# A windowed-attention kernel with two feed-forward layers: the softmax's sum, constant, reciprocal and division of a strip ordered ahead of the next strip's maximum and GpSimd pass in iterations -1 to 9

## The chip, the core and the metric

One core of a Trainium2 chip. The core has five engines with queues of their own, each run in order: TensorE (matrix products, PE in the profile; PEld are its weight loads), VectorE (DVE), ScalarE (ACT), GpSimd (POOL) and SyncE (SP), which here issues all the DMAs. The metric is the time of one execution on the device in microseconds.

## What is computed

Attention over 2 batches, 8 heads, 768 positions with head size 64, then two feed-forward layers over the 1536 resulting rows of 512 with 2048 hidden units. Cut to what matters:

```
k_sum, v_sum = max and mean of k and v over blocks of 32 positions
local  = q k^T / 8 where |i - j| < 16, else -1e9
blocks = q k_sum^T / 8 + log(32)
a = exp([local, blocks] - max);  a = a / (sum(a) + 1e-9)
x = a [v, v_sum]
h = x w_in1;  g = max(h, 0) + alpha * min(h, 0);  x = g w_out1
h = x w_in2;  g = P(h) / (Q(h) + 1e-6);           out = g w_out2
```

## The kernel before, in words

The 2 x 768 queries are cut into 24 strips of 64. A strip's scores, for four pairs of heads at once, are a tile of 128 x 480: 96 local keys and 24 block keys per pair. One iteration of the loop over t (-1 to 27) issues for several strips the steps that a pipeline has them at. The dictionary `attn` gives each step's offset: `qk`, `mask` (scores into SBUF, L402), `max` (L410) and `sub` (subtraction of the maximum, L415, only for strips marked "s" in `SOFTMAX`) work on strip t; `exp` (L420 or L424), `sum` (L429, where ScalarE has not summed already), `guard` (the constant 1e-9, L434 or L436), `inv` (reciprocal, L440) and `norm` (the division as a product, L444) on strip t-1; `turn` (transposes on TensorE, L450) and `turned` (their copy to SBUF, `pT`) on strip t-2 and `vm`, `pv` (product with v, L464), `out` and `outl` (x as a high part `xh` and a rest `xl`, L478) on strip t-3 (from strip 8 on, one iteration later in each). `k` copies the keys of strip t+1 into `kc`.

Between these stand the steps of the first feed-forward layer: `H` (products `h`, L195) from iteration 6 on, `act` (its activation in three pieces, on ScalarE and VectorE: relu L204, factor L137, L208), `gh` and `gl` (a high part and a rest of its result), and `Y` (L258). Weights come as 64-bit words by DMA into `raw` and are split on the way: `new` (`top` on ScalarE, L161), `low` (`cv` on VectorE, L163, after which the next piece's DMA is issued), `hi` (copy on ScalarE), `mid` and `end` (the two halves of the rest `wil` or `wol`, on GpSimd, L173). `top` is one buffer, so the next `top` waits for the `cv` that reads it. The buffers in PSUM of the scores, the transposes and the product with v are single.

The order inside an iteration is written out by hand: `ORDERS` has one list of steps for each stage, and `PHASES` (3, 5, 7, 10, 14) says at which iteration the next list begins. `ENG` has one letter per stage and step for the engine: v VectorE, a ScalarE, p GpSimd. A step's instructions go to the end of their engine's queue; what they wait for is added by the framework from the tiles that they read and write. Behind the loop, from about 145 us on, a second loop runs the rest of both layers.

```python
            for step in ORDERS[sum(t >= at for at in PHASES)].split():
                if step in attn:
                    f, o = attn[step]
                    for n in {t + o, t + o - (o < -1)}:
```

Of the kernel before, what the change touches and what calls it, by code (L numbers as in the profile page):

```python
# [39 lines left out]

PHASES = (3, 5, 7, 10, 14)
ORDERS = (
    ("qk mask k act mid exp max turn gl vmean sum kmax vm end ks out hi low pv inv sub outl Y norm guard turned "
     "v act in act H gh new"),
    ("act qk sum hi mid turn act vm act mask in exp vmean gh gl max pv ks v guard out inv sub low turned k end Y "
     "outl kmax H new norm"),
    ("qk vm exp hi act mask pv mid sum max out Y turn sub inv gl guard in low outl act v vmean k act norm H "
     "turned new ks end kmax gh"),
    ("gh qk act pv ks act act exp out end mask hi k sum gl max vmean outl low kmax turn guard mid Y v vm in sub "
     "inv new turned H norm"),  # L50
    ("ks act end act gh exp qk pv hi out mid v act mask k sum gl max outl sub turn vmean Y kmax low H turned in "
     "new inv vm guard norm"),
    ("vm act act gh act qk exp mask hi sum max pv gl inv sub out k mid v outl in turn turned vmean kmax new low "
# [4 lines left out]

SOFTMAX = 'aaaassasaasssabssssssass'

ENG = {"guard": "vapppv", "k": "vaaaaa", "turned": "aaaaaa", "vm": "aaapaa", "ks": "ppppav", "norm": "vppppp", "sub": "pppppp",
       "gl": "vvvppp", "gh": "vapaaa", "hi": "vaaaaa", "mid": "pvpppp", "end": "pppppp", "out": "aaaaaa", "al": "vavaaa"}

LEAD = (4, 6, 4, 4, 9, 13, 5, 10)
# [6 lines left out]
def kernel(  # L71
# [59 lines left out]
    def eng(step):  # L131
        return {"a": nc.scalar, "v": nc.vector, "p": nc.gpsimd}[ENG[step][sum(now[0] >= t for t in PHASES)]]

# [588 lines left out]
```

## Time and profile before

| | us |
|---|---|
| median of 3 runs | 621.86 (621.47 to 623.15) |
| profiled execution | 620.94 |
| its span, first to last instruction | 618.8 |
| TensorE busy | 594.4 (96%) |
| ScalarE busy | 383.7 (62%) |
| GpSimd busy | 354.8 (57%) |
| VectorE busy | 338.9 (55%) |

Times in the trace count from the start of the span. Busy TensorE is not TensorE at its peak, since its products are pipelined. A row of the timeline gives the start, the duration, the engine, the line, the operation, the tile written and those read, and in square brackets the engine's idle time just before, with what ended it.

### The profile page before, as it was taken

Reading aid. Unit: us, or ns where it says so; the run is one execution under the profiler, and the core shown is the slowest. Engines: PE = TensorE matmul, PEld = TensorE weight load, DVE = VectorE, ACT = ScalarE, POOL = GpSimd, SP = SyncE. Lnnn points to the kernel's source line nnn. Section 1 sums busy time; section 2 is a strip of 40 time slices with the busy share of each in tenths; the row PEclk is TensorE's granted clock in tenths of the full one; section 3 lists DMA queues with packets and bytes.
Section 4 is the critical chain, followed back from the end, with each engine's and each line's share of the span. In section 5 each row is a group of like instructions: output and inputs, shape, how many; then the busy total and the mean of one; then the engine's idle time right before and its main releaser. Section 6 shows DMA issues by size and latency. Waiting matters only on the chain.

```text
span 618.8 us, 8590 instructions
## 1 busy us (share of the span) xinstructions
PE 594.4 (96%) x3192; PEld 496.2 (80%) x3192; DVE 338.9 (55%) x494; ACT 383.7 (62%) x665; POOL 354.8 (57%) x343
## 2 busy tenths in 40 slices
PE   4679999999999999999999999999999999999996
PEld 2567989988888888888888888888888888888884
DVE  4766678654222111144555277776566666566664
ACT  1789798877444333367777467776566666566663
POOL 3266779675622222147777557776466666466662
PEclk9779999999999999999999999999999999999999
DMA  8898576524300000015555101000100000100001
GB/s 298 294 322 285 172 243 226 192 83 151 122 0 2 0 1 1 0 69 187 182 183 197 68 1 68 1 0 2 48 21 1 0 1 1 69 0 2 0 2 68
DMA packets 17129, 55.09 MB, mean 89 GB/s; under 512 B 2368, under 2 KB 4416, under 8 KB 12992
## 3 DMA queue, kind: packets, MB, share of 16 engines
q1 hardware_dynamic: 17088, 54.55, 26.1%
q8 instruction: 25, 0.41, 0.3%
q14 instruction: 16, 0.13, 0.1%
HBM read 51.39 MB, written 3.15 MB: 88 GB/s over the span
## 4 chain that ended last, share of the span: by engine, by line
PE 75%; DVE 10%; ACT 7%; DMA 3%; POOL 2%; issue 2%; SPq 1%; DVEq 0%; ACTq 0%
PE h L195 35%; PE y L258 35%; DVE tp L230 2%; DVE tp L220 2%; DVE h L229 2%; DVE tu L228 2%; ACT h L226 2%; ACT h L227 2%; PE s L394 1%; DVE tp L219 1%; PE po L464 1%; DMA na<-in_pa 1%; DMA raw<-in_w_in 1%; PE pt L450 1%; ACT top L161 1%
## 5 line engine op out<-in xcount | busy, mean ns | idle before, releaser
L195 PE MATMUL h<-xh,wih 128*128 128x512 f32 (+1 forms) x416 | 155.7, 374 | 0.0
L195 PE MATMUL h<-xl,wih 128*128 128x512 f32 (+1 forms) x416 | 155.2, 373 | 0.0
L195 PE MATMUL h<-xh,wil 128*128 128x512 f32 (+1 forms) x416 | 155.0, 373 | 0.0
L242 POOL TENSOR_TENSOR gl<-tp,gh 128x512 fp32r<-128x512 f32 (+1 forms) x75 | 95.2, 1269 | 80.3 <-ACT gh L137 78.9
L137 ACT ACTIVATE gh<-tp 128x512 fp32r<-128x512 f32 (+1 forms) x76 | 46.2, 608 | 91.6 <-DVE tp L230 46.0
L195 PEld LDWEIGHTS h<-xh,wih 128*128 128x128 f32 x416 | 78.3, 188 | 13.9 <-ACT kc L137 0.2
L195 PEld LDWEIGHTS h<-xl,wih 128*128 128x128 f32 x416 | 78.3, 188 | 14.0 <-issue 0.2
L195 PEld LDWEIGHTS h<-xh,wil 128*128 128x128 f32 x416 | 78.4, 188 | 13.8
L258 PE MATMUL y<-gh,woh 128*128 128x512 f32 (+1 forms) x224 | 81.9, 366 | 0.0
L258 PE MATMUL y<-gh,wol 128*128 128x512 f32 (+1 forms) x224 | 80.3, 359 | 0.0
L258 PE MATMUL y<-gl,woh 128*128 128x512 f32 (+1 forms) x224 | 80.3, 359 | 0.0
L258 PE MATMUL y<-woh,gh 128*128 128x512 f32 x192 | 74.8, 390 | 1.1 <-ACT gh L137 1.1
L163 DVE SCALAR_TENSOR_TENSOR cv<-raw,top 128x1024 int32<-128x1024 int32 x32 | 59.2, 1848 | 30.4 <-ACT top L161 23.9
L258 PE MATMUL y<-wol,gh 128*128 128x512 f32 x192 | 74.7, 389 | 0.0
L258 PE MATMUL y<-woh,gl 128*128 128x512 f32 x192 | 74.5, 389 | 0.0
L228 DVE SCALAR_TENSOR_TENSOR tu<-tu,h 128x512 f32<-128x512 f32 x48 | 33.0, 688 | 71.0 <-ACT h L227 67.5
L217 POOL TENSOR_SCALAR tu<-tv,ab 128x512 f32<-128x512 f32 x48 | 37.1, 774 | 58.0 <-ACT tv L215 58.0
L218 POOL TENSOR_TENSOR tu<-tu,tv 128x512 f32<-128x512 f32 x48 | 62.2, 1296 | 4.0
L242 POOL TENSOR_TENSOR gl<-tu,gh 128x512 fp32r<-128x512 f32 (+1 forms) x28 | 33.1, 1184 | 49.9 <-ACT gh L137 49.9
L208 DVE SCALAR_TENSOR_TENSOR tp<-h,tp 128x512 f32<-128x512 f32 (+1 forms) x28 | 17.2, 614 | 69.9 <-ACT tp L137 69.9
L226 ACT ACTIVATE h<-tu,lnb 128x512 f32<-128x512 f32 x48 | 33.2, 692 | 35.1 <-DVE tp L220 32.7
L208 DVE SCALAR_TENSOR_TENSOR tu<-h,tu 128x512 f32<-128x512 f32 (+1 forms) x28 | 17.2, 613 | 60.6 <-ACT tu L137 60.6
(79 smaller groups left out, 1061.4 us busy)
## 6 DMA issues: line engine op xcount, KB each, us to landing
raw<-in_w_in SPq DMA_DIRECT2D x16, 1024.0 KB, 4.8
raw<-in_w_out SPq DMA_DIRECT2D x16, 1024.0 KB, 4.8
qz<-in_qT SPq DMA_DIRECT2D x25, 256.0 KB, 5.3
vc<-in_vS SPq DMA_DIRECT2D x24, 192.0 KB, 5.4
kt<-in_kT SPq DMA_DIRECT2D x16, 208.0 KB, 5.4
vt<-in_vS SPq DMA_DIRECT2D x12, 256.0 KB, 5.1
out<-stage SPq DMA_DIRECT2D x12, 256.0 KB, 2.1
al<-in_alpha SPq DMA_DIRECT2D x1, 8.0 KB, 6.0
```

The costliest lines, as they stand in the source:

```text
L137: e.activation(out=out, in_=in_, func=AF.Copy, scale=1.0 if scale is None else scale)
L163: nc.vector.scalar_tensor_tensor(out=w.bitcast(I32), in0=rest, scalar=13, in1=top, op0=ALU.logical_shift_right, op1=ALU.bitwise_or)
L195: nc.tensor.matmul(out=ps, lhsT=a, rhs=b, start=(c == 0 and m == 0), stop=(c == NC - 1 and m == 2))
L208: nc.vector.scalar_tensor_tensor(out=t, in0=ps, scalar=0.0, in1=t, op0=ALU.max, op1=ALU.subtract)
L217: nc.gpsimd.tensor_scalar(out=q, in0=v, scalar1=ab[:, 1:2], scalar2=ab[:, 0:1], op0=ALU.mult, op1=ALU.add)
L218: nc.gpsimd.tensor_tensor(out=q, in0=q, in1=v, op=ALU.mult)
L220: nc.vector.scalar_tensor_tensor(out=p, in0=p, scalar=na[:, 1:2], in1=ps, op0=ALU.add, op1=ALU.mult)
L226: nc.scalar.activation(out=A, in_=q, func=AF.Ln, scale=2.0 ** -LN_SHIFT, bias=lnb)
L227: nc.scalar.activation(out=A, in_=A, func=AF.Exp, scale=-1.0, bias=exb)
L228: nc.vector.scalar_tensor_tensor(out=q, in0=q, scalar=one, in1=A, op0=ALU.add, op1=ALU.mult)
L242: (eng("gl") if (u, f) != steps[-1] else nc.vector).tensor_tensor(out=gl, in0=t, in1=gh.bitcast(F32), op=ALU.subtract)
L258: nc.tensor.matmul(out=yps[c][:, c0:c0 + n] if layer == 0 else yps[c], lhsT=a, rhs=b, start=(f == 0 and c0 == 0 and m == 0), stop=(f == NF ...
```

## The change

In the first four lists of `ORDERS` (iterations -1 to 9) `guard`, `inv` and `norm` are moved forward: they now follow `exp` and `sum`, in this order, ahead of `max` and `sub` (in the first list they come behind `max`). Before, `norm` stood near the end of each list, and `guard` came behind `inv` in the first and third, so that the reciprocal did not wait for it. In the first list `max` moves ahead of `k`, in the second `exp` goes ahead of `mask` and `vm`, in the third `sum`, `guard`, `inv` and `norm` go ahead of `mask`. `guard` goes from GpSimd to ScalarE in iterations 5 to 9.

```diff
-    ("qk mask k act mid exp max turn gl vmean sum kmax vm end ks out hi low pv inv sub outl Y norm guard turned "
-     "v act in act H gh new"),
-    ("act qk sum hi mid turn act vm act mask in exp vmean gh gl max pv ks v guard out inv sub low turned k end Y "
-     "outl kmax H new norm"),
-    ("qk vm exp hi act mask pv mid sum max out Y turn sub inv gl guard in low outl act v vmean k act norm H "
+    ("qk mask max k exp guard inv norm turn act mid act gl vmean sum kmax vm end ks out hi low pv sub outl Y "
+     "turned v in act H gh new"),
+    ("act qk exp sum hi mid guard inv norm turn act vm act mask in vmean gh gl max pv ks v out sub low turned k "
+     "end Y outl kmax H new"),
+    ("qk vm exp hi act sum guard inv norm mask pv mid max out Y turn sub gl in low outl act v vmean k act H "
      "turned new ks end kmax gh"),
-    ("gh qk act pv ks act act exp out end mask hi k sum gl max vmean outl low kmax turn guard mid Y v vm in sub "
-     "inv new turned H norm"),
+    ("gh qk act pv ks act act exp out end mask hi k sum guard inv gl norm max vmean outl low kmax turn mid Y v "
+     "vm in sub new turned H"),

-ENG = {"guard": "vapppv", "k": "vaaaaa", "turned": "aaaaaa", "vm": "aaapaa", "ks": "ppppav", "norm": "vppppp", "sub": "pppppp",
+ENG = {"guard": "vaaapv", "k": "vaaaaa", "turned": "aaaaaa", "vm": "aaapaa", "ks": "ppppav", "norm": "vppppp", "sub": "pppppp",
```

GpSimd in iterations 5 and 6, first as it was (`wil0` and `wil1` are the rests of the first two weight pieces, L415 is sub, L436 guard, L444 norm; p_378 is strip 4, p_424 strip 5):

```order
L173 TENSOR_TENSOR wil0_422<-cv_364,wih0_421 128x512
L415 TENSOR_TENSOR p_424<-p_424,m_426 128x480
L436 TENSOR_SCALAR d_381<-d_381 128x4
L444 TENSOR_TENSOR p_378<-p_378,d_381 128x480
L173 TENSOR_TENSOR wil0_422<-cv_364,wih0_421 128x512
L173 TENSOR_TENSOR wil1_468<-cv_409,wih1_467 128x512
L436 TENSOR_SCALAR d_427<-d_427 128x4
L444 TENSOR_TENSOR p_424<-p_424,d_427 128x480
```

and as it is in the change (strip 4 is p_385, strip 5 p_428):

```order
L444 TENSOR_TENSOR p_385<-p_385,d_388 128x480
L173 TENSOR_TENSOR wil0_422<-cv_365,wih0_421 128x512
L415 TENSOR_TENSOR p_428<-p_428,m_430 128x480
L173 TENSOR_TENSOR wil0_422<-cv_365,wih0_421 128x512
L444 TENSOR_TENSOR p_428<-p_428,d_431 128x480
```

The division of strip 4 stands in front of the first rest and of the subtraction for strip 5, and the constants are gone from this queue.

VectorE in iterations 6 and 7, as it was (L429 sum, L402 mask, L410 max, L440 inv, L478 outl, L344 a maximum of keys, L208 the last piece of an activation, L163 cv; p_470 is strip 6, p_550 strip 7):

```order
L402 SCALAR_TENSOR_TENSOR p_470<-s_460,bias1_147 128x480
L429 TENSOR_REDUCE d_427<-p_424 128x4
L410 TENSOR_REDUCE m_472<-p_470 128x4
L440 RECIPROCAL d_427<-d_427 128x4
L478 TENSOR_TENSOR xl_94<-po_474,xh_93 128x4x64
L344 TENSOR_REDUCE kmax_360<-kt_277 128x12
L208 SCALAR_TENSOR_TENSOR tu_532<-h_503,tu_532 128x256
L402 SCALAR_TENSOR_TENSOR p_550<-s_527,bias1_147 128x480
L410 TENSOR_REDUCE m_552<-p_550 128x4
L478 TENSOR_TENSOR xl_94<-po_534,xh_93 128x4x64
L163 SCALAR_TENSOR_TENSOR cv_518<-raw_403,top_91 128x1024
L440 RECIPROCAL d_473<-d_473 128x4
```

and in the change (strip 6 is p_474 with d_477):

```order
L429 TENSOR_REDUCE d_431<-p_428 128x4
L440 RECIPROCAL d_431<-d_431 128x4
L402 SCALAR_TENSOR_TENSOR p_474<-s_460,bias1_147 128x480
L410 TENSOR_REDUCE m_476<-p_474 128x4
L478 TENSOR_TENSOR xl_94<-po_478,xh_93 128x4x64
L344 TENSOR_REDUCE kmax_361<-kt_277 128x12
L208 SCALAR_TENSOR_TENSOR tu_532<-h_503,tu_532 128x256
L402 SCALAR_TENSOR_TENSOR p_550<-s_527,bias1_147 128x480
L440 RECIPROCAL d_477<-d_477 128x4
L410 TENSOR_REDUCE m_552<-p_550 128x4
L478 TENSOR_TENSOR xl_94<-po_534,xh_93 128x4x64
L163 SCALAR_TENSOR_TENSOR cv_518<-raw_404,top_91 128x1024
```

The reciprocal of strip 5 moves ahead of the mask of strip 6, and that of strip 6 from behind `cv` to a place ahead of the maximum of strip 7.

ScalarE in iterations 6 and 7, in the change (L434 is the constant, which this queue did not have there; the rest of these rows and their order are as before):

```order
L420 ACTIVATE p_428<-p_428 128x480
L137 ACTIVATE wih1_467<-cv_410 128x1024
L434 ACTIVATE d_431<-d_431 128x4
L137 ACTIVATE xh_93<-po_478 128x4x64
L137 ACTIVATE kc1_182<-kt_204 128x4x96
L137 ACTIVATE pT_516<-pt_490 120x512
L161 ACTIVATE top_91<-raw_404 128x1024
L204 ACTIVATE tu_532<-h_503 128x256
L137 ACTIVATE tu_532<-tu_532,al_83 128x256
L424 ACTIVATE p_474,d_477<-p_474,m_476 128x120 x4
L137 ACTIVATE xh_93<-po_534 128x4x64
L137 ACTIVATE kc0_181<-kt_204 128x4x96
```

The constant of strip 5 stands behind the weight copy and ahead of the copy `xh`; that of strip 6 comes right behind the last of these rows. TensorE and the DMA queue of SyncE keep their order.

## Rows read from the trace of the kernel before

**Rows 1.** Busy time by stretch: stretch, length, busy us of each engine, clock, DMA

```profile
80.00:90.00 10.00, 9.18 (x98) 8.61 (x97) 8.26 (x15) 9.90 (x27) 7.85 (x8) 1.00 0.74 265
```

**Rows 2.** Chain of work that ended last: start us, duration us, what

```profile
24.07 7.23 DMA raw<-in_w_in
...
68.47 0.39 ACT tp L204
```

**Rows 3.** Timeline of TensorE, 24 to 50 us

```profile
24.30 2.07 PE L394 MATMUL s<-kc,qz 128*128 128x120 f32 x8 [2.37 <-ACT kc L137]
...
39.77 0.65 PE L450 MATMUL pt<-ident,p 128*120 128x128 f32 x4 [1.13 <-POOL p L444]
...
41.24 0.28 PE L195 MATMUL h<-xl,wih 128*128 128x256 f32 x1
...
49.49 0.69 PE L464 MATMUL po<-pT,vc 120*64 120x64 f32 x16 [1.48 <-ACT pT L137]
```

**Rows 4.** Timeline of ScalarE, 20 to 48 us

```profile
20.57 0.63 ACT L137 ACTIVATE vc<-vmean 24x512 f32<-24x512 f32 x1
...
22.87 0.21 ACT L434 ACTIVATE d<-d 128x4 f32<-128x4 f32 x1
...
31.38 1.35 ACT L161 ACTIVATE top<-raw 128x1024 f16<-128x1024 bf16 x1 [1.78 <-DMA raw<-in_w_in]
...
34.04 1.04 ACT L137 ACTIVATE wih<-cv 128x1024 fp32r<-128x1024 f32 x1
...
38.40 0.60 ACT L420 ACTIVATE p<-p 128x480 f32<-128x480 f32 x1 [1.40 <-POOL p L415]
...
39.85 0.37 ACT L137 ACTIVATE xh<-po 128x256 fp32r<-128x256 f32 x1
...
42.75 0.38 ACT L204 ACTIVATE tu<-h 128x256 f32<-128x256 f32 x1 [0.36 <-PE h L195]
...
45.09 0.36 ACT L137 ACTIVATE xh<-po 128x256 fp32r<-128x256 f32 x1
45.36 0.51 ACT L137 ACTIVATE kc<-kt 128x384 f32<-128x384 f32 x1
...
47.65 1.35 ACT L161 ACTIVATE top<-raw 128x1024 f16<-128x1024 bf16 x1 [1.78 <-DVE cv L163]
```

**Rows 5.** Timeline of VectorE, 28 to 48 us

```profile
28.42 1.20 DVE L163 SCALAR_TENSOR_TENSOR cv<-raw,top 128x1024 int32<-128x1024 int32 x1
...
31.76 0.66 DVE L402 SCALAR_TENSOR_TENSOR p<-s,bias 128x480 f32<-128x480 f32 x1 [1.81 <-PE s L394]
...
35.30 0.17 DVE L440 RECIPROCAL d<-d 128x4 f32<-128x4 f32 x1
35.38 2.13 DVE L163 SCALAR_TENSOR_TENSOR cv<-raw,top 128x1024 int32<-128x1024 int32 x1
...
40.25 0.42 DVE L478 TENSOR_TENSOR xl<-po,xh 128x256 fp32r<-128x256 f32 x1
...
45.83 1.79 DVE L163 SCALAR_TENSOR_TENSOR cv<-raw,top 128x1024 int32<-128x1024 int32 x1
```

**Rows 6.** Timeline of GpSimd, 35 to 86 us

```profile
35.16 1.27 POOL L173 TENSOR_TENSOR wil<-cv,wih 128x512 fp32r<-128x512 f32 x1 [3.76 <-ACT wih L137]
...
36.39 1.97 POOL L415 TENSOR_TENSOR p<-p,m 128x480 f32<-128x480 f32 x1
...
38.73 0.99 POOL L444 TENSOR_TENSOR p<-p,d 128x480 f32<-128x480 f32 x1
...
45.55 0.99 POOL L415 TENSOR_TENSOR p<-p,m 128x480 f32<-128x480 f32 x1
...
82.03 3.49 POOL L173 TENSOR_TENSOR wol<-cv,woh 128x512 fp32r<-128x512 f32 x2 [1.72 <-ACT woh L137]
```

**Rows 7.** Granted clock by stretch: stretch, length, TensorE busy, clock, DMA share, GB/s

```profile
24.00:25.00 1.00, 0.70 (x3) 0.50 0.98 345
...
37.00:38.00 1.00, 0.82 (x7) 0.74 0.85 289
```

## The prediction

> **What bounds the kernel now.** I read the windows first: between 80 and 90 us TensorE is busy for 9.18 of 10 us at full clock [rows 1], and it stays that dense. From there to the end almost no TensorE time is left to win, so this change can only move the moment at which the dense stretch begins. The chain of waits says when that is settled: up to 31 us it hangs on a DMA, the second weight piece, which lands at 31.3; at 68.5 it runs through ScalarE, released by TensorE itself [rows 2]. Behind 31 us nothing on it is tied to a fixed moment; a delay there is handed on to the end one for one. The timeline of TensorE shows two waits that matter: 1.13 us before the transpose of strip 4, which waits for its division on GpSimd, and 1.48 us before the product of strip 5 with v (49.49), which waits for a copy on ScalarE; the first product with xl starts at 41.24 [rows 3]. The copy comes late because ScalarE stood 1.78 us before `top` (47.65) [rows 4], which waits for VectorE's `cv` (45.83) [rows 5]. I call strip n's steps exp(n), sum(n) and so on; iteration t masks strip t and finishes the softmax of t-1. The i-th `top`, and the `cv` that reads it, I call top#i and cv#i. In rows of VectorE and ScalarE a queued instruction starts about 0.09 us before the recorded end of the one ahead (45.09 with 0.36, next at 45.36) [rows 4].
>
> **Iterations -1 to 4: hidden.** VectorE now does k(t+1) behind max(t), one reduction later, and mask(t) waits for the reciprocal. On ScalarE exp(2) and exp(3) go ahead of the `vm` copy (0.63 us [rows 4]); the pv product (0.69 [rows 3]) that needs it, and the k copy behind that, come some 0.9 us later, by 0.63 plus part of the product's run. ScalarE then waits 1.78 us for the DMA at 31.38 [rows 4], and the issue order of the DMA queue is unchanged. 0.9 fits into 1.78: cost 0. Without that cover it would be 0.9.
>
> **Iteration 5: the pass of strip 5 on GpSimd goes later.** Before, GpSimd ran half a weight residue (35.16), sub(5) (36.39 to 38.36), the constant, norm(4) (38.73) [rows 6]; inv(4) ran ahead of the constant and did not wait for it. Now it is sum(4), guard(4), inv(4), norm(4), then the residue, then sub(5). guard(4) stands on ScalarE behind `hi` (34.04 + 1.04 - 0.09 = 34.99) and takes 0.21 [rows 4]; inv(4) takes 0.17 [rows 5], and with two hand-overs of 0.04 norm(4) starts at 35.45. It holds GpSimd 0.95, the residue 1.25: 37.65. `cv#2`, queued behind max(5) since about 36.5, gets in there for 1.1 us, as it did at 35.38 (2.13 long, of which the first half was waiting) while sub(5) waited behind it and took 1.97 [rows 5, 6]. So sub(5) ends at 37.65 + 1.95 = 39.6, against 38.36: **+1.25**. exp(5) had been waiting for just that (1.40 us idle before 38.40 [rows 4]).
>
> **Iteration 6: VectorE stands behind the constant.** exp(5) and `hi` move by 1.25; guard(5) adds 0.12 of ScalarE, so xh(3) goes from 39.85 to 41.2. On VectorE inv(5) waits for guard(5) (41.3), and mask(6) and max(6), formerly done by then, follow it: 41.35 + 0.08 + 0.57 + 0.56 puts outl(3) at 42.55, against 40.25 [rows 5]. The first product with xl starts at 43.0 against 41.24: **+1.8**. TensorE's 1.13 us wait for norm(4) [rows 3] goes, but that is no gain, since xl is late next; and pv(3) now waits for outl(2), which stands behind `cv#2` in VectorE's queue.
>
> **Iteration 7: the same once more, in front of `cv`.** The first relu (42.75) and xh(4) (45.09) move by 1.8, to 46.9; kc follows, then guard(6) at 47.55, ending 47.77 [rows 4]. VectorE waits: inv(6) 47.8, max(7) 47.9, outl(4) 48.45, `cv#3` queued at 48.8. Formerly `cv#3` was queued at 45.83, waited for sub(7) (45.55 to 46.54) and ended at 47.6 [rows 5, 6], so that it ran for 1.1 once let in. Now norm(6), released by inv(6), holds GpSimd from 48.0 to 49.0; `cv#3` then runs for 1.1 and top#4 starts at 50.1, against 47.65: **+2.45**. The pv product of strip 5 moves from 49.49 to 51.95. TensorE's own work is ready by 49.9, so it does not decide.
>
> Here the rows and a rule have to be weighed. A `cv` took 1.20 where it was not held up (28.42), and at 35.38 2.13 [rows 5]; sub(5), queued on GpSimd directly behind the residue, was the one that waited then, and at 82.03 two residues in a row took 3.49 us where one takes 1.27 [rows 6], so that about one us was let in between them. A waiting VectorE gets the gap, and I take +2.45. The Trainium skill, page "SBUF — State Buffer", section "Who interferes with whom", says that a VectorE instruction with two SBUF inputs and a GpSimd instruction that reads SBUF exclude each other, and that issue order decides who blocks. The trace agrees with the exclusion; by issue order alone sub(7), queued in front of `cv#3`, could go first, which would add its 1.0 and make +3.45.
>
> **Iterations 8 and 9.** Relative to the shifted start, ScalarE gets two more constants, guard(7) and guard(8), of 0.12 each: +0.25, since its queue is nearly gapless there and TensorE's pv(7) has under 0.2 us to spare (an estimate from the spacing above). GpSimd loses its constants there, which nobody waits for. max(8) and max(9) come later behind the reciprocal, but exp(8) and exp(9) are later still in ScalarE's queue: 0. From iteration 10 both orders agree.
>
> **Sum.** 0 + 2.45 + 0.25 = **+2.7 us**. On the profiled execution, 620.94 us, that is 623.6; that execution lies 0.9 below the median of the three runs, 621.86, and on the median the forecast is **624.6 us**. Unknown costs: who gets the gap (0 or +1.0), and what the constant costs ScalarE (0.12 queued, 0.21 recorded, five times: at most +0.45 in all). Below, the waiting of VectorE could be shorter by a hand-over or two: -0.5.
>
> **The rivals.**
> - *TensorE's clock falls once more: +4.7, 626.6.* After 2.37 us of idleness (before 24.30 [rows 3]) the granted clock stood at half, 0.50 in the slice from 24 us: 1.2 GHz instead of 2.4 [rows 7]. My schedule has a gap of about 2.05 us before 51.95. For it: it is nearly as long. Against it: the gap of 1.48 before 49.49 comes in a stretch at full clock. The clock came back in the slice from 37 us (0.74 [rows 7]), 13 us later. How long it would stay down here I can only bound, by 13 us from above; I take four us of products at half pace, an estimate, which lose 2.0. The Trainium skill, page "TensorE: Matmul & The Clock Gate", section "What's actually happening", says the same of an idle stretch and a sustained busy one; the fall in the rows agrees. Chance 0.15.
> - *Only the second stall counts: +1.2, 623.1.* If sub(5) is not pushed back (the residue or `cv#2` running elsewhere), what is left is guard, inv and max in front of `cv#3`: 0.21 + 0.17 + 0.57, plus 0.25. Against it: GpSimd's new queue has norm(4) in front in any case. Chance 0.20.
> - *Not slower: the earlier divisions win, -1.1 to -1.8, about 620.* TensorE's 1.13 us before the transpose goes, and `cv#3` meets no GpSimd instruction, which saves the 0.7 by which 1.79 exceeds 1.1. It decides if outl(3) ends by 41.1, that is, if exp(5) starts no later than at 38.4, so if the constant on ScalarE is free and sub(5) still ends by 38.4. Chance 0.12.
>
> That the change does not take hold is excluded: VectorE, GpSimd and ScalarE run in another order, while TensorE and the DMA queue keep theirs.
>
> **How the numbers follow.** Forecast (+2.0 to +3.6) 0.53, the rivals 0.15, 0.20 and 0.12. 0.3% (1.9 us) is about what a measurement of this kernel can tell from no change. Slower: 0.53 + 0.15 = 0.68. Within 0.3%: the +1.2 case and part of the last, 0.25. Faster: 0.07. The range leaves out most of the last case below and little above: 621.5 (-0.4) to 627.5 (+5.6, the clock with the lost gap).
>
> **What would show it.** In the changed profile sub(5) should end near 39.6, outl(3) start near 42.5, the top that waits for `cv` start near 50.1 after an idle ScalarE of about 2 us, and the pv product of strip 5 near 52; each shift should stand in the next. Wrong would be: exp(5) starting near 38.4; a first xl product before 42; a half clock behind 43 us; or those shifts in place and the end not moved.

## The result and the profile after

The change takes 625.23 us (median of 4 runs, 624.93 to 626.20) beside 621.66 for the kernel before (4 runs, 621.33 to 623.15): a ratio of 1.0055 [1.0035, 1.0075], or 3.6 us slower. The forecast was 624.6 on a median of 621.86, so +2.7. The profiled execution took 625.10, with a span of 623.1 against 618.8.

The page, its busy times:

```profile
PE 597.3 (96%) x3192; PEld 497.8 (80%) x3192; DVE 338.2 (54%) x494; ACT 384.0 (62%) x670; POOL 355.8 (57%) x338
```

The work is the same: ScalarE and GpSimd are busy 0.3 and 1.0 us more, VectorE 0.7 less, and TensorE 2.9 more with the products that it had. The dense stretch is the same too, 9.17 us of TensorE in ten, as in [rows 1]:

```profile
80.00:90.00 10.00, 9.17 (x98) 8.60 (x97) 6.66 (x11) 8.55 (x24) 5.44 (x6) 1.00 0.59 185
```

So the time is lost ahead of it. The timeline of ScalarE shows where, row by row beside [rows 4]:

```profile
31.82 0.52 ACT L137 ACTIVATE kc<-kt 128x384 f32<-128x384 f32 x1
32.25 1.34 ACT L161 ACTIVATE top<-raw 128x1024 f16<-128x1024 bf16 x1
...
40.50 0.60 ACT L420 ACTIVATE p<-p 128x480 f32<-128x480 f32 x1 [2.65 <-POOL p L415]
...
41.95 0.19 ACT L434 ACTIVATE d<-d 128x4 f32<-128x4 f32 x1
...
46.10 0.38 ACT L204 ACTIVATE tu<-h 128x256 f32<-128x256 f32 x1 [1.53 <-PE h L195]
...
49.11 0.19 ACT L434 ACTIVATE d<-d 128x4 f32<-128x4 f32 x1
...
51.79 1.35 ACT L161 ACTIVATE top<-raw 128x1024 f16<-128x1024 bf16 x1 [2.48 <-DVE cv L163]
```

Each row that has a partner in [rows 4] is later than it, and by more each time: `top`#2 by 0.87 (31.38 to 32.25), exp(5) by 2.10 (38.40), the first relu by 3.35 (42.75), `top`#4 by 4.14 (47.65). The span is 4.3 us longer. ScalarE's wait for strip 5 on GpSimd grew from 1.40 to 2.65, that for `cv` from 1.78 to 2.48. The 1.78 of waiting for the DMA ahead of `top`#2 is gone, because the copy of the keys ahead of it on ScalarE ends only then.

GpSimd and VectorE show what ScalarE waits for, first GpSimd:

```profile
36.33 0.99 POOL L444 TENSOR_TENSOR p<-p,d 128x480 f32<-128x480 f32 x1 [3.84 <-DVE d L440]
37.27 1.27 POOL L173 TENSOR_TENSOR wil<-cv,wih 128x512 fp32r<-128x512 f32 x1
38.50 1.97 POOL L415 TENSOR_TENSOR p<-p,m 128x480 f32<-128x480 f32 x1
...
49.69 0.99 POOL L444 TENSOR_TENSOR p<-p,d 128x480 f32<-128x480 f32 x1 [3.78 <-DVE d L440]
50.63 1.97 POOL L415 TENSOR_TENSOR p<-p,m 128x480 f32<-128x480 f32 x1
```

and VectorE:

```profile
37.39 2.23 DVE L163 SCALAR_TENSOR_TENSOR cv<-raw,top 128x1024 int32<-128x1024 int32 x1
...
42.17 0.18 DVE L440 RECIPROCAL d<-d 128x4 f32<-128x4 f32 x1 [0.39 <-ACT d L434]
42.27 0.64 DVE L402 SCALAR_TENSOR_TENSOR p<-s,bias 128x480 f32<-128x480 f32 x1
42.95 0.66 DVE L410 TENSOR_REDUCE m<-p 128x4 f32<-128x480 f32 x1
43.52 0.41 DVE L478 TENSOR_TENSOR xl<-po,xh 128x256 fp32r<-128x256 f32 x1
...
49.34 0.18 DVE L440 RECIPROCAL d<-d 128x4 f32<-128x4 f32 x1 [1.30 <-ACT d L434]
49.44 0.62 DVE L410 TENSOR_REDUCE m<-p 128x4 f32<-128x480 f32 x1
49.97 0.42 DVE L478 TENSOR_TENSOR xl<-po,xh 128x256 fp32r<-128x256 f32 x1
50.30 1.45 DVE L163 SCALAR_TENSOR_TENSOR cv<-raw,top 128x1024 int32<-128x1024 int32 x1
```

The division of strip 4 runs ahead of the residue and sub(5), which ends at 40.47. VectorE stands idle for the constant at 42.17 with mask(6), max(6) and outl(3) behind it, and again at 49.34 with max(7), outl(4) and `cv`#3. This is the forecast's sequence, each step later than forecast by the 0.87 of `top`#2 or more: sub(5) ends at 40.47 (39.6 was forecast), outl(3) starts at 43.52 (42.5), `top`#4 at 51.79 (50.1), and the product of strip 5 with v at 53.63 (52).

Two things were not in it. The first is the late `top`#2. The products ahead of it come later from strip 1 on. The product with the keys of strip 2, which started at 16.67 before, waits for VectorE, where the copy of these keys now runs behind a maximum (at 17.34, it was 15.99); the row names `d`, which VectorE wrote directly behind that copy:

```profile
17.34 0.35 DVE L139 COPY kc<-kt 128x384 f32<-128x384 f32 x1
...
17.79 1.12 PE L394 MATMUL s<-kc,qz 128*128 128x120 f32 x8 [0.96 <-DVE d L436]
```

Then TensorE waits for ScalarE's copies of the mean of v and of the keys, four times up to 33 us. In sum that is 5.36 us, no more than its waits of 2.37 [rows 3], 1.38 and 1.84 before, but the copies come later:

```profile
23.97 0.69 PE L464 MATMUL po<-pT,vc 120*64 120x64 f32 x16 [1.65 <-ACT vc L137]
...
26.17 2.06 PE L394 MATMUL s<-kc,qz 128*128 128x120 f32 x8 [1.52 <-ACT kc L137]
...
29.77 1.12 PE L464 MATMUL po<-pT,vc 120*64 120x64 f32 x16 [0.68 <-ACT vc L137]
...
32.40 2.06 PE L394 MATMUL s<-kc,qz 128*128 128x120 f32 x8 [1.51 <-ACT kc L137]
...
53.63 0.69 PE L464 MATMUL po<-pT,vc 120*64 120x64 f32 x16 [2.28 <-ACT pT L137]
```

before:

```profile
29.66 2.06 PE L394 MATMUL s<-kc,qz 128*128 128x120 f32 x8 [1.38 <-DVE cv L163]
...
33.56 1.12 PE L464 MATMUL po<-pT,vc 120*64 120x64 f32 x16 [1.84 <-ACT vc L137]
```

The second thing is one that the prediction named as a sign of being wrong, a half clock behind 43 us. The granted clock stays at 1.2 GHz to 45 us, where it was back at 2.4 from 38 on before ([rows 7] show 0.74 in the slice from 37). That the change does this is not shown: in e6 and e8 below, whose code is that of the kernel before up to iteration 6, it stays down into the slice from 45 us or to 46 us as well. Stretch, length, busy us of each engine, clock, DMA:

```profile
44.00:45.00 1.00, 1.00 (x5) 1.00 (x5) 0.39 (x1) 0.57 (x1) 1.00 (x2) 0.50 1.03 295
45.00:46.00 1.00, 1.00 (x9) 1.00 (x9) 0.00 (x0) 0.00 (x0) 0.91 (x1) 0.94 1.08 281
```

### The profile page after: what moved, and what is told of

Its sections match the earlier page's. It is cut to its first block, busy times and chain, and to the rows that moved or that the text cites. A ratio compares the mean times of both kernels' runs of the same rounds, so it can differ in the third digit from the quotient of the medians.

```text
span 623.1 us, 8593 instructions
## 1 busy us (share of the span) xinstructions
PE 597.3 (96%) x3192; PEld 497.8 (80%) x3192; DVE 338.2 (54%) x494; ACT 384.0 (62%) x670; POOL 355.8 (57%) x338
## 4 chain that ended last, share of the span: by engine, by line
PE 74%; DVE 10%; ACT 9%; DMA 3%; issue 2%; POOL 1%; SPq 1%; DVEq 0%; ACTq 0%
PE h L195 35%; PE y L258 34%; DMA kt<-in_kT 2%; DVE tp L230 2%; DVE tp L220 2%; DVE h L229 2%; PE s L394 2%; DVE tu L228 2%; ACT h L226 2%; ACT h L227 2%; PE po L464 1%; DVE tp L219 1%; PE pt L450 1%; ACT top L161 1%; DMA qz<-in_qT 1%
## 5 line engine op out<-in xcount | busy, mean ns | idle before, releaser
L163 DVE SCALAR_TENSOR_TENSOR cv<-raw,top 128x1024 int32<-128x1024 int32 x32 | 58.3, 1822 | 30.1 <-ACT top L161 23.5
L208 DVE SCALAR_TENSOR_TENSOR tp<-h,tp 128x512 f32<-128x512 f32 (+1 forms) x28 | 17.2, 614 | 70.0 <-ACT tp L137 70.0
L208 DVE SCALAR_TENSOR_TENSOR tu<-h,tu 128x512 f32<-128x512 f32 (+1 forms) x28 | 17.2, 614 | 61.1 <-ACT tu L137 61.1
```

The costliest lines, as they stand in the source:

```text
L163: nc.vector.scalar_tensor_tensor(out=w.bitcast(I32), in0=rest, scalar=13, in1=top, op0=ALU.logical_shift_right, op1=ALU.bitwise_or)
L208: nc.vector.scalar_tensor_tensor(out=t, in0=ps, scalar=0.0, in1=t, op0=ALU.max, op1=ALU.subtract)
```

## The experiments

My theory after the result: two stalls, one in list 3 (sub(5) behind the division, VectorE behind the constant) and one in list 4 (max(7), outl(4) and `cv`#3 behind the constant), in series. Rival A: the constant on ScalarE is what costs, not the order. Rival B: the clock is what costs; the stalls only matter as far as they keep it low. Rival C, added after the first four: the loss arises ahead of `top`#2, by the `vm` copy behind exp.

All timed results in one table. The kernel before was timed beside each group, with medians of 622.54 (e1 to e4), 623.06 (e5, e6), 622.19 (e7 to e9) and 622.82 (e10 to e12). The ratio and its interval are taken from all runs, so the ratio differs a little from the quotient of the medians:

| | kernel | median, us | ratio to before |
|---|---|---|---|
| e1 | lists 1 and 2 alone | 621.59 | 0.9990 [0.9975, 1.0006] |
| e2 | lists 3 and 4, constant on ScalarE | 625.04 | 1.0035 [1.0024, 1.0046] |
| e3 | four lists, constant on GpSimd | 625.65 | 1.0051 [1.0034, 1.0067] |
| e4 | constant on ScalarE alone | 620.91 | 0.9978 [0.9963, 0.9993] |
| e5 | list 3 alone | 622.95 | 1.0004 [0.9990, 1.0017] |
| e6 | list 4 alone | 624.33 | 1.0018 [1.0008, 1.0029] |
| e7 | change, `vm` ahead of exp in list 2 | 625.63 | 1.0051 [1.0033, 1.0070] |
| e8 | before, `low` early in list 4 | 621.75 | 0.9989 [0.9977, 1.0001] |
| e9 | change, `low` early in list 4 | 622.91 | 1.0011 [1.0000, 1.0022] |
| e10 | e8 and constant on ScalarE | 620.63 | 0.9976 [0.9962, 0.9991] |
| e11 | before, TensorE kept busy | 621.28 | 0.9975 [0.9963, 0.9987] |
| e12 | change, TensorE kept busy | 624.71 | 1.0035 [1.0022, 1.0048] |

### The order or the constant's engine: e1 to e4

e1 is the kernel before with the first two lists of the change:

```diff
-    ("qk mask k act mid exp max turn gl vmean sum kmax vm end ks out hi low pv inv sub outl Y norm guard "
+    ("qk mask max k exp guard inv norm turn act mid act gl vmean sum kmax vm end ks out hi low pv sub outl Y "
-    ("act qk sum hi mid turn act vm act mask in exp vmean gh gl max pv ks v guard out inv sub low turned k end "
+    ("act qk exp sum hi mid guard inv norm turn act vm act mask in vmean gh gl max pv ks v out sub low turned "
```

> Only the first two lists are changed (iterations -1 to 4). My theory (the cost is the sum of stalls on one chain): ScalarE reaches the second top at about 32.2 instead of 31.4, since the cover of 1.78 us is used up, and that is handed on: +0.9, or up to +1.6 if TensorE's half clock lasts longer as it does in the changed kernel. Rival A (the constant on ScalarE is the cost): 0, since no constant moves here. Rival B (the longer half clock is the whole cost): +3.6 if half clock lasts to 45 us, 0 if it ends at 37.5.

e2 has the two other lists, and the constant's engine:

```diff
-    ("qk vm exp hi act mask pv mid sum max out Y turn sub inv gl guard in low outl act v vmean k act norm H "
+    ("qk vm exp hi act sum guard inv norm mask pv mid max out Y turn sub gl in low outl act v vmean k act H "
-    ("gh qk act pv ks act act exp out end mask hi k sum gl max vmean outl low kmax turn guard mid Y v vm in "
+    ("gh qk act pv ks act act exp out end mask hi k sum guard inv gl norm max vmean outl low kmax turn mid Y v "
-ENG = {"guard": "vapppv", "k": "vaaaaa", "turned": "aaaaaa", "vm": "aaapaa", "ks": "ppppav", "norm": "vppppp", "sub": "pppppp",
+ENG = {"guard": "vaaapv", "k": "vaaaaa", "turned": "aaaaaa", "vm": "aaapaa", "ks": "ppppav", "norm": "vppppp", "sub": "pppppp",
```

> Only the third and fourth lists and the constant's engine are changed (iterations 5 to 9). My theory: the second top stays at 31.4, sub of strip 5 ends near 39.6, the top that waits for cv starts near 50.1 and the end is +2.7; the half clock ends at 37.5 as before. Rival A: +3.6, as the whole change. Rival B: 0 if the half clock ends at 37.5.

e3 is the change with the constant left on GpSimd:

```diff
-ENG = {"guard": "vaaapv", "k": "vaaaaa", "turned": "aaaaaa", "vm": "aaapaa", "ks": "ppppav", "norm": "vppppp", "sub": "pppppp",
+ENG = {"guard": "vapppv", "k": "vaaaaa", "turned": "aaaaaa", "vm": "aaapaa", "ks": "ppppav", "norm": "vppppp", "sub": "pppppp",
```

> All four lists are changed, but the constant stays on GpSimd in iterations 5 to 9. My theory: the order costs, not the engine; the constant of strip 6 is done some 0.5 us earlier, since it no longer stands behind two copies on ScalarE, and ScalarE is 0.25 shorter in iterations 8 and 9: +2.8 in place of +3.6 to the kernel before. Rival A: 0 to +0.5. Rival B: +3.6 as long as the half clock lasts to 45 us.

e4 is the kernel before with the opposite of that line: its lists, and the constant on ScalarE.

> The lists of the kernel before; only the constant moves to ScalarE in iterations 5 to 9. My theory: the reciprocals and divisions wait for nothing new, five constants of 0.12 us in ScalarE's queue: 0 to +0.5. Rival A: +3.6. Rival B: 0, with the half clock ending at 37.5.

Measured: e1 0.9990, e2 1.0035, e3 1.0051, e4 0.9978. Rival A falls twice: the order without the constant's move loses about as much as the change, and the constant's move alone gains 1.6 us (622.54 to 620.91). Most of the loss comes with lists 3 and 4 (e2 is 2.5 us above the kernel before), and lists 1 and 2 alone cost nothing that can be measured; what they add to 3 and 4 is not clear of the noise. Two expectations of my theory were missed: +0.9 for e1, and 0 to +0.5 for e4.

A part of e4's gain is in its trace, here VectorE, GpSimd and ScalarE:

```profile
46.26 1.22 DVE L163 SCALAR_TENSOR_TENSOR cv<-raw,top 128x1024 int32<-128x1024 int32 x1
...
46.34 1.98 POOL L415 TENSOR_TENSOR p<-p,m 128x480 f32<-128x480 f32 x1 [3.15 <-DVE xl L478]
...
43.19 0.38 ACT L204 ACTIVATE tu<-h 128x256 f32<-128x256 f32 x1 [1.25 <-PE h L195]
...
47.51 1.37 ACT L161 ACTIVATE top<-raw 128x1024 f16<-128x1024 bf16 x1 [1.11 <-DVE cv L163]
```

Before, sub(7) began at 45.55, 0.28 ahead of `cv`, which then needed 1.79 [rows 5, 6]. In e4 sub(7) begins 0.08 behind `cv`: `cv` runs for 1.22, and sub(7) is the one that waits (1.98 instead of 0.99). From the relu to `top`#4 it is 4.32 us instead of 4.90. sub(7) had slack, `cv` had none. That is 0.58 of the 1.6 us; the rest is not explained, and the two profiled executions themselves are equally long (620.97 and 620.94). How the constant decides which of the two begins first was not tried by itself, and the margin is small. In e5 (below), which still has it on GpSimd in this iteration, 0.08 us later behind the relu than before (2.61 against 2.53), `cv` is short as well. And `cv`#1, up to which e2, e4, e5, e6, e8 and e10 run the code of the kernel before, was let in ahead of the subtraction on GpSimd in some profiles (1.19 to 1.20 long before and in e2, e6 and e10, where it began 0.15 earlier) and not in others (1.80 to 1.96 in e4, e5 and e8, where it began 0.11 to 0.27 later). So who is first also changes without any edit.

### Each list alone: e5 and e6

Lists 3 and 4 of e2 apart, each with its letter of the constant ("vaappv" and "vapapv"). The list of e5:

```diff
-    ("qk vm exp hi act mask pv mid sum max out Y turn sub inv gl guard in low outl act v vmean k act norm H "
+    ("qk vm exp hi act sum guard inv norm mask pv mid max out Y turn sub gl in low outl act v vmean k act H "
```

> Only the third list is changed, with the constant on ScalarE in iterations 5 and 6. My theory (two stalls that add up): the first stall alone, exp of strip 5 at +1.25, the first product with xl at +1.8, the end at +1.8 at an equal granted clock. Rival A (the constant on ScalarE): 2/5 of the whole, +1.4, with exp of strip 5 where it was. Rival B (the half clock is the whole cost): 0 at an equal granted clock.

and of e6:

```diff
-    ("gh qk act pv ks act act exp out end mask hi k sum gl max vmean outl low kmax turn guard mid Y v vm in "
+    ("gh qk act pv ks act act exp out end mask hi k sum guard inv gl norm max vmean outl low kmax turn mid Y v "
```

> Only the fourth list is changed, with the constant on ScalarE in iterations 7 to 9. My theory: the second stall alone, exp of strip 5 where it was, the top that waits for cv +0.7 later, the end +0.7 to +0.9 at an equal granted clock. Rival A: 3/5 of the whole, +2.1. Rival B: 0 at an equal granted clock.

Measured: e5 1.0004 and e6 1.0018. The second stall shows in the time (+1.3 by the medians, where 0.7 to 0.9 was expected), the first does not, where my theory had +1.8. The trace explains e5 only in part. ScalarE in e5:

```profile
30.84 1.35 ACT L161 ACTIVATE top<-raw 128x1024 f16<-128x1024 bf16 x1 [1.65 <-DMA raw<-in_w_in]
...
39.11 0.60 ACT L420 ACTIVATE p<-p 128x480 f32<-128x480 f32 x1 [2.66 <-POOL p L415]
...
44.26 0.38 ACT L204 ACTIVATE tu<-h 128x256 f32<-128x256 f32 x1 [1.07 <-PE h L195]
...
48.59 1.36 ACT L161 ACTIVATE top<-raw 128x1024 f16<-128x1024 bf16 x1 [1.21 <-DVE cv L163]
```

and in e6, whose code is that of the kernel before up to the relu:

```profile
31.91 1.35 ACT L161 ACTIVATE top<-raw 128x1024 f16<-128x1024 bf16 x1 [2.31 <-DMA raw<-in_w_in]
...
38.91 0.60 ACT L420 ACTIVATE p<-p 128x480 f32<-128x480 f32 x1 [1.39 <-POOL p L415]
...
45.69 0.38 ACT L204 ACTIVATE tu<-h 128x256 f32<-128x256 f32 x1 [2.08 <-PE h L195]
...
51.37 1.35 ACT L161 ACTIVATE top<-raw 128x1024 f16<-128x1024 bf16 x1 [2.46 <-DVE cv L163]
```

From `top`#2 to exp(5) the list does what was forecast: 8.27 us in e5, 7.00 in e6. But from `top`#2 to the relu e6 takes 13.78, against 11.37 in the profiled execution of before: same instructions in the same order, but the clock stood at 1.2 GHz to 45 us instead of 37. e5 takes 13.42. So half a clock that lasts long delays the first relu by itself by up to 2.4 us, the stall of list 3 by about two, and the two cover each other instead of adding. e5 also has the gain of e4: `cv` gets ahead of sub(7), and relu to `top`#4 takes 4.33. That the two together make up all of the missing 1.8 us in the timed runs is my reading and not shown; only the two profiles were seen.

### The front: e7

The change, with `vm` ahead of exp again in list 2:

```diff
-    ("act qk exp sum hi mid guard inv norm turn act vm act mask in vmean gh gl max pv ks v out sub low turned k "
+    ("act qk vm exp sum hi mid guard inv norm turn act act mask in vmean gh gl max pv ks v out sub low turned "
```

> The whole change, but in the second list vm stays ahead of exp. My theory: the pv product and the k copy behind it are no longer late in iterations 3 and 4, the second top starts at 31.4 again, and 0.9 of the +3.6 goes: +2.7, or less if the half clock ends earlier as well. Rival A: +3.6, the constants are where they were. Rival B: +3.6 if the half clock still lasts to 45 us.

Measured: 625.63, as slow as the change; the 0.9 that was expected back did not come. The edit worked where it was made: the k copy ahead of `top`#2 comes at 29.81 instead of 31.82. But `top`#2 moved by 0.48 only, to 31.77, because now it waits for VectorE, which has to read the `top` buffer for `cv`#1 first. In the change that `cv`#1 starts at 30.42 (28.42 before [rows 5]), since the reciprocal, the mask and the maximum stand in front of it and the reciprocal waits for the constant; in e7 it starts at 30.53. First two rows of VectorE in the change, then ScalarE in e7:

```profile
29.10 0.18 DVE L440 RECIPROCAL d<-d 128x4 f32<-128x4 f32 x1 [1.62 <-ACT d L434]
...
30.42 1.21 DVE L163 SCALAR_TENSOR_TENSOR cv<-raw,top 128x1024 int32<-128x1024 int32 x1
...
31.77 1.36 ACT L161 ACTIVATE top<-raw 128x1024 f16<-128x1024 bf16 x1 [1.44 <-DVE cv L163]
```

And TensorE's clock fell a second time:

```profile
54.00:55.00 1.00, 1.00 (x3) 0.37 (x2) 1.00 (x3) 1.00 (x3) 0.00 (x0) 0.50 0.96 387
```

It had been idle for 2.27 us before the product of strip 5 at 52.67. From there to the end e7 takes 570.8 against 569.5 in the change, which had the same gap (2.28) and no fall. So e7 does not decide on rival C: it gives back 0.48 of the front's 0.87, and its profile has the product of strip 5 0.96 earlier than the change, and the slow clock behind it costs 1.4. Against rival C speaks e1, which has the front alone and is not slower. What the front is worth by itself stays open.

### Taking the second stall away: e8, e9 and e10

`low` (VectorE's `cv`) directly behind `hi`, ahead of the sum, the constant and the maximum; e8 from the kernel before, e9 from the change:

```diff
-    ("gh qk act pv ks act act exp out end mask hi k sum gl max vmean outl low kmax turn guard mid Y v vm in "
+    ("gh qk act pv ks act act exp out end mask hi low k sum gl max vmean outl kmax turn guard mid Y v vm in "
...
-    ("gh qk act pv ks act act exp out end mask hi k sum guard inv gl norm max vmean outl low kmax turn mid Y v "
+    ("gh qk act pv ks act act exp out end mask hi low k sum guard inv gl norm max vmean outl kmax turn mid Y v "
```

> The kernel before with one word moved: in the fourth list low stands behind hi, so that VectorE runs cv ahead of max in iterations 7 to 9. My theory (ScalarE's top waits for cv, and TensorE for the copy behind that top): top starts near 45.9 instead of 47.65, the pv product of strip 5 near 48.0, where TensorE's own work ends: -1.5. Rival (the chain is another and this wait is covered): 0.

> The changed kernel with the same word moved in its fourth list: cv no longer stands behind the reciprocal and the maximum. My theory: the second stall goes, top starts near 49.3 instead of 51.8, the pv product of strip 5 at 51.4 instead of 53.6: -2.2 to the changed kernel, +1.4 to the kernel before. Rival A: +3.6 to the kernel before, unchanged. Rival B: +3.6, if the half clock lasts to 45 us.

Measured: 621.75 and 622.91, ratios 0.9989 and 1.0011. The same step gains the kernel before 0.4 us on the median and the change 2.3 (from 625.23, which was timed beside another group, at 621.66 for the kernel before), and what is left between e9 and e8, timed together, is 1.2 of the 3.6 us. So most of the loss hangs on `cv`#3 and what stands ahead of it in VectorE's queue. How large the second stall is does not follow from this, since the step takes away more than the change added there: the 0.79 of the change, and 1.79 that the kernel before had already. In both, `top`#4 follows the relu after 3.1 us, without a wait on ScalarE, where it was 4.90 before and 5.69 in the change; here in e9:

```profile
45.65 0.38 ACT L204 ACTIVATE tu<-h 128x256 f32<-128x256 f32 x1 [1.53 <-PE h L195]
...
48.76 1.39 ACT L161 ACTIVATE top<-raw 128x1024 f16<-128x1024 bf16 x1
```

Why e8 gives 0.4 for the 1.79 that it saves there (1.5 was expected) is not settled. In its profile the clock stood at 1.2 GHz to 46 us and the relu came 13.80 behind `top`#2, as in e6.

e10 is e8 with the constant on ScalarE ("vaaapv"), the two gains together:

> The kernel before with two edits: the constant on ScalarE in iterations 5 to 9, and low behind hi in the fourth list. Each alone was about 1 us faster than the kernel before at an equal granted clock. If they remove different waits (GpSimd's queue, and VectorE's cv behind the maximum): -2 at an equal clock. If both act through the same wait for cv: -1.

Measured: 620.63, 0.9976 [0.9962, 0.9991], the best median of the study. It beats the change, and the kernel before by 2.2 us on the median (1.5 by the ratio). From e4 (0.9978) it can't be told apart, so whether the two gains add stays open.

### The clock: e11 and e12

The kernel before and the change, each with 59 more products on TensorE, in the waits up to iteration 8, into a tile that nothing reads:

```diff
+    KEEP = {(3, "turn"): 6, (3, "pv"): 9, (4, "turn"): 5, (4, "pv"): 8, (5, "qk"): 14, (5, "turn"): 5, (6, "pv"): 5, (8, "qk"): 7}
...
+                nc.tensor.matmul(out=idle[:, 0:P], lhsT=ident, rhs=ident, start=True, stop=True)
...
+                            keep(t, step)
```

> The kernel before with 59 products of the identity with itself in TensorE's gaps of iterations 3 to 8, into a PSUM bank that is free there; nothing reads them. They are to keep the granted clock from falling. If half clock costs 0.2 us per us, as the runs so far suggest (a fit over all of them): -2 to -3, less what the added products delay. If the half clock is covered by waits: 0.

> The changed kernel with the same added products. My theory (stalls on VectorE, GpSimd and ScalarE, which the clock does not touch): the gap to the kernel before with the same products stays at +2.5. Rival B (the change costs through a longer half clock): the gap goes to 0 to +0.5.

Measured: 621.28 and 624.71, ratios 0.9975 and 1.0035, at a mean granted clock of 0.996 to 1.0 in all runs of both. e11 gains 1.5 us on the kernel before, where 2 to 3 less a delay was expected. The difference of the two medians is 3.4 us, as without the products (3.6). Rival B falls: at a full clock throughout, the change loses as much. ScalarE in e11:

```profile
33.06 1.36 ACT L161 ACTIVATE top<-raw 128x1024 f16<-128x1024 bf16 x1 [3.42 <-DMA raw<-in_w_in]
...
44.45 0.38 ACT L204 ACTIVATE tu<-h 128x256 f32<-128x256 f32 x1 [0.36 <-PE h L195]
...
49.35 1.37 ACT L161 ACTIVATE top<-raw 128x1024 f16<-128x1024 bf16 x1 [1.78 <-DVE cv L163]
```

and in e12:

```profile
32.12 1.36 ACT L161 ACTIVATE top<-raw 128x1024 f16<-128x1024 bf16 x1 [0.46 <-DMA raw<-in_w_in]
...
45.51 0.38 ACT L204 ACTIVATE tu<-h 128x256 f32<-128x256 f32 x1 [1.04 <-PE h L195]
...
51.21 1.36 ACT L161 ACTIVATE top<-raw 128x1024 f16<-128x1024 bf16 x1 [2.48 <-DVE cv L163]
```

This pair measures the two stalls without the clock: `top`#2 to relu 11.39 and 13.39 (+2.00), relu to `top`#4 4.90 and 5.70 (+0.80). From the product of strip 5 to the end of the span it is 569.29 and 569.54 (+0.25). Sum 3.05. `top`#2 itself waited for its DMA in both, so the front costs nothing in this pair of profiles. In e11 that DMA came late, 0.94 behind e12's, so the two spans differ by 2.1 only (620.5 and 622.6); e11's profiled execution took 622.64, 1.4 more than its median.

## Why the prediction was right

By its steps:

- *sub(5) later by 1.25.* Right in place and size: `top`#2 to exp(5) is 7.02 before and 8.25 after (+1.23), and 7.00 to 7.03 or 8.25 to 8.28 in the other kernels, by whether they have the new list 3. `cv`#2 got GpSimd's gap, as taken: 2.23 long at 37.39, and sub(5) took 1.97 behind it.
- *First product with xl +1.8.* Counted from `top`#2 it starts +1.88 later in the change (43.99 against 41.24, less 0.87) and +1.90 at a full clock (e12 against e11); to the relu that is +2.00 (e12). The constant and the reciprocal in front of mask(6) cost what was added up: outl(3) starts 3.02 after exp(5), where it was 1.85.
- *`top`#4 +2.45, so +0.65 more.* Measured +0.79 in the change and +0.80 at full clock. The gap question went as taken: `cv`#3 started at 50.30 and ended at 51.75, sub(7), queued at 50.63, took 1.97. The Trainium skill, page "SBUF — State Buffer", section "Who interferes with whom", lets issue order decide who blocks. The trace agrees if the moment counts at which an operation stands at the head of its queue: sub(7) in the kernel before began first and held `cv` up (1.79 long [rows 5]), and in the change `cv`#3, waiting since 50.30, got in ahead of sub(7), whose turn in GpSimd's queue came at 50.63. The +3.45 of the prediction would have needed the place in the queue to decide.
- *Iterations 8 and 9 +0.25.* Measured +0.25 (e12) and +0.16 (569.47 against 569.31, change and before).
- *The sum +2.7.* The mechanism's part is 3.05 by e11 and e12, and within the 3.6 and 3.4 of the timed runs; the bounds of the range held. The addition of the two stalls is shown at a full clock only. With the clock as it mostly is, "a delay there is handed on to the end one for one" did not hold for list 3 alone (e5), so that the total comes as close there is in part luck.

One step failed: **"Iterations -1 to 4: hidden ... cost 0"**. The delay was put at 0.9, once, under a cover of 1.78. In the changed profile it is 2.74, in three parts. ScalarE's copy of the mean of v out of PSUM starts at 20.34 instead of 19.35: that is VectorE's copy of the keys behind the maximum, which the prediction named and put at nothing. The k copy of iteration 3 comes at 25.60 instead of 23.73, that of iteration 4 at 31.82 instead of 29.08: that is the `vm` copy behind exp, once in each. So the last ends at 32.34 instead of 29.60 (31.38 less its wait of 1.78 [rows 4]), which uses up the cover and puts `top`#2 0.87 later. Without the `vm` part `cv`#1, which ends at 31.63 behind the reciprocal and its constant, would have held `top`#2 beyond 31.38 as well, as e7 shows; the prediction put that wait of VectorE at nothing, too. In that execution the front is a fifth of the span's 4.3. What it is worth in the timed runs is not settled: e1 shows no cost (0.9990 [0.9975, 1.0006]), although its profiled execution (623.72, beside a slowest run of 624.27) has a late `top`#2 without a wait, at 32.80. `top`#2 starts anywhere from 30.84 (e5) to 33.06 (e11) where it waits for its DMA; a late one would hide the front as forecast, but that was seen in profiles only.

The profile's 4.3 are then 0.87 (front), 1.23 (sub(5)), 1.25 (exp(5) to relu: 0.65 up to the first product with xl, behind the constant, and 0.60 from there on, with the clock at 1.2 GHz, where it is 0.10 at a full clock), 0.79 (`cv`#3) and 0.16 (end).

Of the rivals, the one in which the earlier divisions win failed at its own condition: exp(5) started at 40.50, not by 38.4. The constant's move, which it needed to be free, gains by itself (e4). "Only the second stall counts" is nearer than its 0.20 says: with the clock as it mostly is, list 3 alone costs nothing that can be measured. The clock rival did not decide (e12), but what it describes happened: in e2, e3 and e7 the clock fell once more behind the gap before the product of strip 5, and the stretch from there to the end is 1.4 us longer than in the change, where I had put 2.0.

## What to carry to other kernels

A step on a strip that has slack (a division that nobody waits for yet) should not be put in front of one without (the maximum, the part `xl`, the weight piece) on an engine with an in-order queue: here the cost of the two stalls, at a full clock, could be added up from the rows queued behind each wait. Where VectorE and GpSimd hold each other up, look at which of two simultaneous operations has slack, and let the other start first. In e4, with 0.2 us instructions moved out of GpSimd's queue, `cv` did start first and the kernel gained 1.6 us; that the one is the cause of the other is shown for 0.58 at most. A stall can be worth less than its length where another one, or a slow clock, ends at the same moment (e5 beside e6), so measure parts alone and in pairs.

## What was not expected

The kernel before scatters from 619.5 to 624.6 us over the 93 runs that were timed beside the experiments, and that goes in part with its mean granted clock: 619.5 to 621.7 in the 15 runs where that is 0.991, 622.6 to 624.6 in the 22 where it is 0.982 to 0.984, but 621.4 to 623.8 in the 49 at 0.986. So the time that TensorE spends at 1.2 GHz varies from run to run of one program, and the profiled execution of before (620.94, 0.988) was a quick one. Whether the clock makes the time, or the waits make both, is not shown. With 59 useless products the clock was at full throughout, and the kernel before became 0.25% faster [0.13%, 0.37%], though not faster than its own runs at 0.991. Of stretch, length, busy us, clock, DMA in e11,

```profile
25.00:26.00 1.00, 1.00 (x12) 1.00 (x11) 0.55 (x1) 0.97 (x2) 0.00 (x0) 1.00 1.03 233
```

against 0.50 in that slice before and in the change. The same gap did not always do the same: 2.28 us of idleness ahead of 53.63 in the change left the clock at 1.00 in the slice from 54, 2.27 ahead of 52.67 in e7 did not, and in e3 it fell behind 1.83 ahead of 52.82.
